# One overlapping transfer for eight shifted value tiles, a new order of the first loads, a third gate and up buffer, and zero matmuls between the first ones

## The chip, the cores and the metric

The kernel runs on one core of a Trainium2 chip. The core has five engines, each with its own instruction stream that runs in order: TensorE (PE; weight loads are listed apart as PEld), VectorE (DVE), ScalarE (ACT), GpSimd (POOL) and SyncE (SP), which here only issues transfers. The metric is the device time of one execution in microseconds (us), as the median of six runs.

## The reference

Sequence 2048, width D = 640, 32 heads of 20, window of 8 positions that lie 2 apart; F = 1536; bfloat16.

```python
xn = layernorm(x)                                  # (x - mean) / sqrt(var + 1e-5)
q, k, v = split(xn @ wqkv)                         # 32 heads of 20
logits[s, w] = q[s] . k[s - 2w] * 20**-0.5         # w = 0..7; s - 2w < 0 is masked out
o[s] = sum_w softmax_w(logits)[s, w] * v[s - 2w]
attention = o @ wo
glu = ((xn @ w_gate) * (xn @ w_up)) @ w_down       # bilinear: no nonlinearity
out = x + attention + glu
```

## The kernel before

The 2048 positions are 16 tiles of 128 (`tg`), in four chunks of four tiles (512 positions, `c`). All weights are loaded to SBUF once. For each chunk the stages are:

- `norm(c)`: DVE takes the statistics of each x tile (`stats`, `mv`), POOL makes 1/sigma (`rstd`), DVE scales (`xn`), PE turns the tile (`pst`) and ACT copies it to `xnT`. Chunk 0 goes tile by tile, so that on DVE the statistics of tile 2 stand ahead of `xn` of tile 1; the other chunks go by four tiles.
- `qk(c)` and `vproj(c)`: PE projects (`psqk`, `psv`), ACT copies to `qT`, `kT`, `v_t`. v goes out to a DRAM buffer `vD`, which begins with 14 rows of zeros (HALO). From there `load_v8(tg)` brings back, for each tile, eight copies of v, each shifted by two rows more, as one SBUF tile `v8` (two buffers).
- `weights(c)`: DVE multiplies q by eight shifted views of k (`pw`, eight products per chunk), PE sums over each head (`lps`), ACT takes the exponential (`e`).
- `attend(c)`: per tile PE turns the weights (`eT`), DVE normalises them (`rs`, `a`), multiplies the eight v copies by them (the mix, L481), and adds them up in three steps to `o`; PE turns `o` (`pso`), ACT copies it to `oT`.
- `glu(c)`: 12 column blocks f. For each, PE makes gate (`psg`) and up (`psu`), five matmuls each, ACT copies them to `gs` and `us` (two buffers each), DVE multiplies them to `hT`.
- `finish(c)`: per tile and half, PE adds attention output and down projection into `psf` (5 and 12 matmuls), DVE adds the residual `xr`, which POOL loads, into `osb`, and a transfer writes it out.

A hand-written list builder sets the order. `main` holds PE's stages and `chain` DVE's; `burst` and `quick` are short operations that are put in between when a table of estimated times says that they are ready. `later` holds transfers that are issued once a named step is done in that table (`want_v8`). The result is one fixed order per engine. On the chip an engine that waits holds back everything behind it in that order; SP too issues its transfers strictly in order. A name such as `v_599` is one buffer of `v8`, with a number that differs between tiles and between the two kernels.

Of the kernel before, what the change touches and what calls it, by code (L numbers as in the profile page):

```python
# [9 lines left out]
BF = dt.bfloat16  # L10
# [7 lines left out]
def kernel(  # L18
# [60 lines left out]
    def tcols(ttl):  # L79
        return slice(ttl * P, (ttl + 1) * P)  # L80
# [7 lines left out]

    x_tiles = {}

    def load_x(c):
        for ttl in range(CH):
            tg = c * CH + ttl
            x_t = cpool.tile([P, D], BF, name="x_t", bufs=6)
            nc.sync.dma_start(out=x_t[:], in_=x_flat[tg * P : (tg + 1) * P, :])
            x_tiles[tg] = x_t
# [7 lines left out]
            out=wqkv[:, :, r * D : (r + 1) * D], in_=wqkv_r[:, :, r * D : (r + 1) * D]  # L104
        )

    load_x(0)
    load_qkv(2)
    load_qkv(0)
    load_x(1)  # L110
    load_qkv(1)
# [20 lines left out]
    def constants():  # L132
        identity(P + H)
        for wl in range(JL):
            nc.gpsimd.affine_select(
                out=selb[:, P : P + H], in_=selb[:, P : P + H], pattern=[[-1, H]],
                compare_op=ALU.not_equal, fill=1.0, base=-H * wl, channel_multiplier=1,
            )
        nc.gpsimd.memset(Ek[:], 1.0)
        nc.gpsimd.affine_select(  # L140
            out=Ek[:], in_=Ek[:], pattern=[[P, KT], [-Dh, H]],
            compare_op=ALU.is_ge, fill=0.0, base=0, channel_multiplier=1,
        )
        nc.gpsimd.affine_select(
            out=Ek[:], in_=Ek[:], pattern=[[-P, KT], [Dh, H]],
            compare_op=ALU.is_ge, fill=0.0, base=Dh - 1, channel_multiplier=-1,
        )
        nc.gpsimd.memset(vmask[:], 1.0)
        for w in range(1, W):
            g, wl = divmod(w, JL)  # L150
            nc.gpsimd.memset(vmask[wl * H : (wl + 1) * H, g, 0 : DIL * w], 0.0)
        zt = cpool.tile([P, D], BF, name="zt", tag="osb")
        nc.gpsimd.memset(zt[0:HALO, :], 0.0)
        nc.gpsimd.dma_start(out=vD[0:HALO, :], in_=zt[0:HALO, :])
# [9 lines left out]
            nc.sync.dma_start(out=wo_perm[jl * H : (jl + 1) * H, :, :], in_=wo_r[jl])  # L164
        nc.sync.dma_start(out=wd[:], in_=B_w_down.rearrange("(f p) d -> p f d", p=P))

    wps = ps_log.tile([P, CS], F32, name="wps", tag="lg")
    for k in range(42):
        nc.tensor.matmul(wps[:, 0:P], lhsT=warm[:], rhs=warm[:], start=True, stop=True)

    INF = 1e9
    LAG = 0.2
# [53 lines left out]
    def norm(c, group):  # L226
        st = state[c]
        st["xnT"] = None

        def alloc():  # L230
            if st["xnT"] is None:
                st["xnT"] = cpool.tile([P, KT, CS], BF, name="xnT", bufs=3)

        def steps(t0):
            g = {}

            def stats():
                g["mv"] = cpool.tile([P, group, nc.vector.BN_AGGR_DIM], F32, name="mv", bufs=2)
                for k in range(group):
                    x_t = x_tiles[c * CH + t0 + k]  # L240
                    s = cpool.tile([P, 2, nc.vector.BN_STATS_DIM], F32, name="stats")
                    for hf in range(2):
                        nc.vector.bn_stats(s[:, hf, :], x_t[:, hf * N2 : (hf + 1) * N2])  # L243
                    nc.vector.bn_aggr(g["mv"][:, k, :], s[:])
                rstd = cpool.tile([P, group], F32, name="rstd", bufs=2)
                nc.gpsimd.tensor_scalar(rstd[:], g["mv"][:, :, 1], EPS, None, op0=ALU.add)
                nc.gpsimd.tensor_tensor(
                    rstd[:], rstd[:], mhalf[:].to_broadcast([P, group]), ALU.pow
                )
                g["rstd"] = rstd  # L250

            def stats_after(t):
                on("pool", ("rstd", c, t0), t + LAG, 0.85)

            op(chain, ("stats", c, t0), stats, 1.12 * group, None, stats_after)

            def scaling(ttl, k):
                def scale_x():
                    xn_t = cpool.tile([P, D], BF, name="xn_t")
                    nc.vector.tensor_scalar(  # L260
                        xn_t[:], x_tiles[c * CH + ttl][:],
                        scalar1=g["mv"][:, k, 0:1], scalar2=g["rstd"][:, k : k + 1],
                        op0=ALU.subtract, op1=ALU.mult,
                    )
                    st["xn", ttl] = xn_t

                def turn():
                    alloc()
                    pst = ps_tr.tile([P, KT, P], BF, name="pst", tag="tr")
                    for i in range(KT):  # L270
                        nc.tensor.transpose(  # L271
                            pst[:, i, :], st["xn", ttl][:, i * P : (i + 1) * P], ident
                        )
                    nc.scalar.copy(st["xnT"][:, :, tcols(ttl)], pst[:])

                def turned(t):
                    on("act", ("xnT", c, ttl), t + LAG, 0.7)

                def scaled(t):
                    op(burst, ("turn", c, ttl), turn, 0.3, when(("xn", c, ttl)), turned,  # L280
                       ("tr", ("xnT", c, ttl)), 0.5)

                def later_free():
                    old = ("turn", c, ttl - 2)
                    return max(done.get(("rstd", c, t0), INF), done.get(old, INF) if ttl >= 2 else 0.0)

                op(chain, ("xn", c, ttl), scale_x, 0.43, later_free, scaled)

            return [lambda k=k: scaling(t0 + k, k) for k in range(group)]

        if group == 1:
            prev = None
            for t0 in range(CH):
                cur = steps(t0)
                if prev:
                    prev[0]()
                prev = cur
            prev[0]()
        else:
            for t0 in range(0, CH, group):  # L300
                for f in steps(t0):
                    f()
# [70 lines left out]
    def load_v8(tg):  # L373
        c, ttl = divmod(tg, CH)
        v8 = apool.tile([P, W, D], BF, name="v8")
        for w in range(W):
            r0 = HALO + tg * P - DIL * w
            nc.sync.dma_start(out=v8[:, w, :], in_=vD[r0 : r0 + P, :])
        state[c]["v8", ttl] = v8
        done["v8", tg] = max(done["v", c, ttl, 1] + 2.5, done.get(("add1", tg - 2), 0.0)) + 5.0  # L380

# [5 lines left out]
    def weights(c):  # L387
        st = state[c]
        for g in range(2):
            for j in range(JL):  # L390

                def product(g=g, j=j):
                    off = HALO - DIL * (JL * g + j)
                    pt = apool.tile([P, KT, CS], BF, name="pw", tag="pw", bufs=6)
                    nc.vector.tensor_tensor(  # L395
                        pt[:], st["qT"][:], st["kT"][:, :, off : off + CS], ALU.mult
                    )
                    st["pw", g, j] = pt
# [28 lines left out]
    def attend(c, ttls):  # L427
# [29 lines left out]
        for ttl in ttls:  # L457
# [44 lines left out]
            def turn(ttl=ttl):  # L502
                o16 = st["o16", ttl]
                pso = ps_tr.tile([P, KT, P], BF, name="pso", tag="tr")
                for i in range(KT):
                    nc.tensor.transpose(pso[:, i, :], o16[:, i * P : (i + 1) * P], ident)  # L506
                oT = cpool.tile([P, KT, P], BF, name="oT", bufs=6)
                nc.scalar.copy(oT[:], pso[:])  # L508
                st["oT", ttl] = oT

# [1 line left out]
                on("act", ("oT", tg), t + LAG, 0.7)  # L512

            def mixed(t, tg=tg, turn=turn, turned=turned):
                old = ("pe fin", (tg - 6), 1)
                need = when(("add1", tg), *([old] if tg >= 6 else []))
                op(burst, ("turn o", tg), turn, 0.3, need, turned, ("tr", ("oT", tg)), 0.5)
                want_v8(tg + 2)

# [7 lines left out]
    def glu(c):  # L527
        st = state[c]
        for f in range(FT):
            for r in range(2):  # L530

                def emit(f=f, r=r):
                    w = wu if r else wg
                    ps = mm_tile("psu" if r else "psg")
                    for i in range(KT):
                        nc.tensor.matmul(  # L536
                            ps[:], lhsT=w[:, i, f * P : (f + 1) * P], rhs=st["xnT"][:, i, :],
                            start=(i == 0), stop=(i == KT - 1),
                        )
                    s = cpool.tile([P, CS], BF, name="us" if r else "gs", bufs=2)  # L540
                    nc.scalar.copy(s[:], ps[:])  # L541
                    st["gu", r, f] = s

# [10 lines left out]
                        op(quick, ("h", c, f), gate, 0.42, when(("gu", c, f, 1)))  # L554

                n = c * FT + f - 14
                need = [("h", c, f - 2)] if f >= 2 else []
                op(main, ("pe gu", c, f, r), emit, 1.08, when(*need), after, ("mm", ("gu", c, f, r)))

    def finish(c):  # L560
# [62 lines left out]
    )  # L623
    norm(1, 4)
    weights(0)
    side(lambda: (want_v8(0), want_v8(1), load_x(3)))
    norm(2, 4)
    attend(0, range(CH))
    weights(1)
    norm(3, 4)  # L630
    attend(1, range(CH))
# [52 lines left out]
```

## Time and profile before

| what | value |
|---|---|
| median of six runs | 289.16 us (287.37 to 290.72) |
| profiled execution | 288.73 us, span 287.0 us |
| granted TensorE clock, mean | 0.987 |
| moved by DMA | 40.96 MB, mean 143 GB/s |

The span runs from the first to the last instruction of the program; the rest of the execution's time lies around it. In lists of waits the columns are: who waited, for whom, us in total, times, longest. In timelines: start, duration, engine, line, operation, tiles, shapes, count, and in brackets the idle time ahead of it with what ended it. A group of matmuls shows a duration somewhat longer than its place in the stream, since the next group begins before its last results are out; the distance from start to start tells what it takes. In rows of windows the columns are the stretch, its length, the busy time of PE, PEld, DVE, ACT and POOL (with counts), the granted clock, the busy share of the DMA engines and GB/s.

### The profile page before, as it was taken

What the parts mean: (1) busy time and instruction counts of PE and PEld (TensorE: products, weight loads), DVE (VectorE), ACT (ScalarE), POOL (GpSimd) and SP (SyncE); (2) the same over time, 40 slices, a digit from 0 to 9 for tenths busy, and PEclk for the clock granted to TensorE, in tenths of its full rate; (3) what the DMA queues carried; (4) which work ended last, traced back from release to release, by engine and by line L of the source; (5) the groups of instructions that cost most, each with busy time, mean ns of one, the idle gap of its engine ahead of it and who ended that gap; (6) DMA issues with size and microseconds to landing.
All of it is one profiled execution on the core that took longest, in us unless ns stands there. A gap on an engine that the chain in (4) does not pass through costs nothing.

```text
span 287.0 us, 4601 instructions
## 1 busy us (share of the span) xinstructions
PE 273.9 (95%) x1778; PEld 155.1 (54%) x1778; DVE 197.6 (69%) x278; ACT 118.5 (41%) x209; POOL 34.7 (12%) x80
## 2 busy tenths in 40 slices
PE   7799999949999999999999999999999999999994
PEld 6554446514444577744444576654445775444773
DVE  5630894199999839999995996995999931211221
ACT  2466555624565521055555640025554003555000
POOL 4710004000000142100000041120000122000100
PEclk9799999997999999999999999999999999999999
DMA  6959993926666122776600485860066022000111
GB/s 212 337 174 382 280 312 119 315 75 183 184 185 183 48 69 70 216 223 202 182 4 3 123 270 178 252 206 26 0 181 188 23 74 88 0 0 2 43 51 47
DMA packets 30758, 40.96 MB, mean 143 GB/s; under 512 B 3298, under 2 KB 29424, under 8 KB 30736
## 3 DMA queue, kind: packets, MB, share of 16 engines
q1 hardware_dynamic: 28736, 33.93, 38.4%
q0 software_dynamic: 2000, 6.74, 7.1%
q8 instruction: 14, 0.23, 0.3%
q14 instruction: 8, 0.07, 0.1%
HBM read 35.39 MB, written 5.26 MB: 142 GB/s over the span
## 4 chain that ended last, share of the span: by engine, by line
PE 62%; DVE 26%; DMA 7%; issue 2%; SPq 1%; ACT 1%; POOL 1%; DVEq 0%; ACTq 0%
PE psf L584 14%; PE psqk L325 11%; PE psg L536 10%; PE psu L536 10%; PE psv L351 6%; PE psf L577 6%; DVE pw L395 5%; PE lps L406 3%; DMA wqkv<-in_A_wqkv_dram 2%; DVE hT L546 2%; DMA v_599<-vD 2%; DMA xr<-in_A_x_dram 2%; PE pst L271 1%; DVE osb L591 1%; DVE stats L243 1%
## 5 line engine op out<-in xcount | busy, mean ns | idle before, releaser
L536 PE MATMUL psg<-xnT,wg 128*128 128x512 bf16 x240 | 60.7, 384 | 0.0
L536 PE MATMUL psu<-xnT,wu 128*128 128x512 bf16 x240 | 59.9, 380 | 0.0
L584 PE MATMUL psf<-wd,hT 128*128 128x320 bf16 x384 | 57.7, 299 | 0.5 <-DVE hT L546 0.5
L395 DVE TENSOR_TENSOR pw<-qT,kT 128x2560 bf16<-128x2560 bf16 x32 | 46.0, 1484 | 0.7 <-PE lps L406 0.7
L584 PEld LDWEIGHTS <-hT 128*128 128x128 bf16 x384 | 37.5, 98 | 15.3 <-DVE hT L546 0.8
L541 ACT CAST gs<-psg 128x512 bf16<-128x512 f32 x48 | 28.2, 588 | 40.6 <-PE psg L536 32.5
L325 PE MATMUL psqk<-xnT,wqkv 128*128 128x512 bf16 x200 | 44.8, 379 | 0.0
L546 DVE TENSOR_TENSOR hT<-gs,us 128x512 bf16<-128x512 bf16 x48 | 20.2, 420 | 27.3 <-ACT us L541 27.3
L536 PEld LDWEIGHTS <-wu 128*128 128x128 bf16 x240 | 23.3, 98 | 27.7 <-issue 1.7
L541 ACT CAST us<-psu 128x512 bf16<-128x512 f32 x48 | 28.3, 589 | 24.1 <-PE psu L536 24.1
L536 PEld LDWEIGHTS <-wg 128*128 128x128 bf16 x240 | 23.4, 99 | 26.7 <-issue 1.2
L591 DVE TENSOR_TENSOR osb<-psf,xr 128x320 bf16<-128x320 f32 x32 | 15.3, 487 | 26.1 <-PE psf L584 17.0
L325 PEld LDWEIGHTS <-wqkv 128*128 128x128 bf16 x200 | 19.2, 98 | 22.4 <-issue 0.8
L351 PE MATMUL psv<-wqkv,xnT 128*128 128x320 bf16 x160 | 24.7, 310 | 2.4 <-DMA wqkv<-in_A_wqkv_dram 2.4
L577 PE MATMUL psf<-wo_perm,oT 128*128 128x320 bf16 x160 | 27.0, 299 | 0.0
L508 ACT COPY oT<-pso 128x640 bf16<-128x640 bf16 x16 | 11.1, 696 | 35.5 <-PE pso L506 35.5
L351 PEld LDWEIGHTS <-xnT 128*128 128x128 bf16 x160 | 15.7, 101 | 9.8 <-issue 2.8
L601 POOL DMA_DIRECT2D out_dram<-osb x13 | 7.1, 546 | 105.5 <-DVE osb L591 105.5
L577 PEld LDWEIGHTS <-oT 128*128 128x128 bf16 x160 | 15.3, 98 | 5.7
L357 ACT CAST v_t<-psv 128x320 bf16<-128x320 f32 x32 | 13.5, 427 | 11.7 <-PE psv L351 9.4
L363 POOL DMA_DIRECT2D vD<-v_t x12 | 6.7, 559 | 93.4 <-ACT v_t L357 93.3
L331 ACT CAST qT<-psqk 128x512 bf16<-128x512 f32 x20 | 11.8, 588 | 9.8 <-PE psqk L325 9.8
(136 smaller groups left out, 236.4 us busy)
## 6 DMA issues: line engine op xcount, KB each, us to landing
x_t<-in_A_x_dram SPq DMA_DIRECT2D x16, 160.0 KB, 7.1
xr<-in_A_x_dram POOLq DMA_DIRECT2D x16, 160.0 KB, 2.7
wqkv<-in_A_wqkv_dram SPq DMA_DIRECT2D x3, 800.0 KB, 7.4
out_dram<-osb POOLq DMA_DIRECT2D x13, 160.0 KB, 2.1
wg<-in_B_w_gate_dram SPq DMA_DIRECT2D x2, 960.0 KB, 7.2
wu<-in_B_w_up_dram SPq DMA_DIRECT2D x2, 960.0 KB, 9.3
wd<-in_B_w_down_dram SPq DMA_DIRECT2D x1, 1920.0 KB, 11.8
vD<-v_t POOLq DMA_DIRECT2D x12, 160.0 KB, 2.4
```

Of the source, the lines that this page charges most:

```text
L325: nc.tensor.matmul(ps[:], lhsT=wqkv[:, i, r * D + j * P : r * D + (j + 1) * P], rhs=st["xnT"][:, i, :], start=(i == 0), stop=(i == KT - 1),)
L331: nc.scalar.copy(dst[:, j, o : o + CS], ps[:])
L351: nc.tensor.matmul(ps[:, 0:N2], lhsT=st["xnT"][:, i, tcols(ttl)], rhs=wqkv[:, i, 2 * D + n0 : 2 * D + n0 + N2], start=(i == 0), stop=(i == ...
L357: nc.scalar.copy(v_t[:].rearrange("p (j h) -> p j h", j=Dh)[:, :, k * HH : (k + 1) * HH], ps[:, 0:N2].rearrange("p (h j) -> p j h", j=Dh),)
L395: nc.vector.tensor_tensor(pt[:], st["qT"][:], st["kT"][:, :, off : off + CS], ALU.mult)
L508: nc.scalar.copy(oT[:], pso[:])
L536: nc.tensor.matmul(ps[:], lhsT=w[:, i, f * P : (f + 1) * P], rhs=st["xnT"][:, i, :], start=(i == 0), stop=(i == KT - 1),)
L541: nc.scalar.copy(s[:], ps[:])
L546: nc.vector.tensor_tensor(h[:], st["gu", 0, f][:], st["gu", 1, f][:], ALU.mult)
L577: nc.tensor.matmul(ps[:, 0:N2], lhsT=st["oT", ttl][:, i, :], rhs=wo_perm[:, i, n0 : n0 + N2], start=(i == 0), stop=False,)
L584: nc.tensor.matmul(ps[:, 0:N2], lhsT=st["hT", f][:, tcols(ttl)], rhs=wd[:, f, n0 : n0 + N2], start=False, stop=(f == FT - 1),)
L591: nc.vector.tensor_tensor(osb[:, n0 : n0 + N2], ps[:, 0:N2], xr[:, n0 : n0 + N2], ALU.add)
```

## The change

- `load_v8` fetches the eight shifted copies by one transfer with an overlapping source pattern (128 rows x 8 shifts x 640) instead of eight transfers. Shift number w now is the one of 14 - 2w rows back, so the views of k and the mask of the first 14 positions run in the opposite order. The bytes moved are the same.
- The first loads: of chunk 0's x tiles two go ahead of the V third of wqkv and two behind it; before, all four went ahead.
- Chunk 3's x tiles are loaded behind attention 0 on the chain instead of ahead of normalisation 2.
- `gs` and `us` have three buffers instead of two (the builder holds gate and up of block f until `hT` of f - 3 instead of f - 2), `oT` five instead of six.
- `warm_up(n)`: the 42 matmuls of zeros at the start stay, and 14 more of the same kind follow the first turned tile.

```diff
-    def load_x(c):
-        for ttl in range(CH):
+    def load_x(c, ttls=range(CH)):
+        for ttl in ttls:
...
-    load_x(0)
+    load_x(0, (0, 1))
     load_qkv(2)
+    load_x(0, (2, 3))
     load_qkv(0)
     load_x(1)
     load_qkv(1)
...
-        for w in range(1, W):
+        for w in range(W - 1):
             g, wl = divmod(w, JL)
-            nc.gpsimd.memset(vmask[wl * H : (wl + 1) * H, g, 0 : DIL * w], 0.0)
+            nc.gpsimd.memset(vmask[wl * H : (wl + 1) * H, g, 0 : HALO - DIL * w], 0.0)
...
+    def warm_up(n):
+        wps = ps_log.tile([P, CS], F32, name="wps", tag="lg")
+        for k in range(n):
+            nc.tensor.matmul(wps[:, 0:P], lhsT=warm[:], rhs=warm[:], start=True, stop=True)
+    warm_up(42)
...
                     nc.scalar.copy(st["xnT"][:, :, tcols(ttl)], pst[:])
+                    if c == ttl == 0:
+                        warm_up(14)
...
-        for w in range(W):
-            r0 = HALO + tg * P - DIL * w
-            nc.sync.dma_start(out=v8[:, w, :], in_=vD[r0 : r0 + P, :])
+        rows = vD[tg * P : (tg + 1) * P, :]
+        nc.sync.dma_start(
+            out=v8[:],
+            in_=bass.AP(tensor=rows.tensor, offset=rows.offset, ap=[[D, P], [DIL * D, W], [1, D]]),
+        )
...
-                    off = HALO - DIL * (JL * g + j)
+                    off = DIL * (JL * g + j)
...
-                oT = cpool.tile([P, KT, P], BF, name="oT", bufs=6)
+                oT = cpool.tile([P, KT, P], BF, name="oT", bufs=5)
...
-                    s = cpool.tile([P, CS], BF, name="us" if r else "gs", bufs=2)
+                    s = cpool.tile([P, CS], BF, name="us" if r else "gs", bufs=3)
...
-                need = [("h", c, f - 2)] if f >= 2 else []
+                need = [("h", c, f - 3)] if f >= 3 else []
...
     weights(0)
-    side(lambda: (want_v8(0), want_v8(1), load_x(3)))
+    side(lambda: (want_v8(0), want_v8(1)))
     norm(2, 4)
     attend(0, range(CH))
+    side(lambda: load_x(3))
     weights(1)
```

How the order of instructions moves. On SP behind the other weights (wo_perm and wd are those of the output and down projections), before:

```order
L164 DMA wo_perm<-in_A_wo_dram 32x5x640 x4
L165 DMA wd<-in_B_w_down_dram 128x12x640
L95 DMA x_t<-in_A_x_dram 128x640 x4
L378 DMA v_599<-vD 128x640 x8
L378 DMA v_608<-vD 128x640 x8
```

and after:

```order
L165 DMA wo_perm<-in_A_wo_dram 32x5x640 x4
L166 DMA wd<-in_B_w_down_dram 128x12x640
L383 DMA v_606<-vD 128x8x640
L383 DMA v_608<-vD 128x8x640
L383 DMA v_849<-vD 128x8x640
L383 DMA v_933<-vD 128x8x640
L383 DMA v_1009<-vD 128x8x640
L383 DMA v_1085<-vD 128x8x640
L95 DMA x_t<-in_A_x_dram 128x640 x4
```

Chunk 3's four x loads moved from ahead of the first v8 transfer to behind the sixth (tile 5, `v_1085`), and each tile is one transfer.

On DVE, where the statistics of chunk 3 end and finish 0 begins, before:

```order
L244 BN_AGGR mv<-stats 128x2
L260 TENSOR_SCALAR xn_t<-x_t,mv,rstd 128x640 x2
L591 TENSOR_TENSOR osb<-psf,xr 128x320 x2
L260 TENSOR_SCALAR xn_t<-x_t,mv,rstd 128x640 x2
L463 RECIPROCAL rs<-eT 128x32
```

and after:

```order
L248 BN_AGGR mv<-stats 128x2
L599 TENSOR_TENSOR osb<-psf,xr 128x320
L264 TENSOR_SCALAR xn_t<-x_t,mv,rstd 128x640
L599 TENSOR_TENSOR osb<-psf,xr 128x320
L264 TENSOR_SCALAR xn_t<-x_t,mv,rstd 128x640
L599 TENSOR_TENSOR osb<-psf,xr 128x320
L264 TENSOR_SCALAR xn_t<-x_t,mv,rstd 128x640 x2
```

The residual additions, which need `xr`, moved ahead of the scalings of chunk 3.

On DVE in finish 1, where the first residual addition stands, before (the mix of tile 10, `v_1975`):

```order
L463 RECIPROCAL rs<-eT 128x32
L465 TENSOR_TENSOR a_2077<-eT,rs 128x256
L481 TENSOR_TENSOR v_1975<-v_1975,a_2077 128x5120
L496 TENSOR_TENSOR v_1975<-v_1975 128x2560
L591 TENSOR_TENSOR osb<-psf,xr 128x320
```

and after (the mix of tile 9, `v_1709`):

```order
L471 RECIPROCAL rs<-eT 128x32
L473 TENSOR_TENSOR a_1978<-eT,rs 128x256
L489 TENSOR_TENSOR v_1709<-v_1709,a_1978 128x5120
L504 TENSOR_TENSOR v_1709<-v_1709 128x2560
L504 TENSOR_TENSOR v_1709<-v_1709 128x1280
L599 TENSOR_TENSOR osb<-psf,xr 128x320
```

The first residual addition of finish 1 now comes about one tile of attention earlier in DVE's order.

More of the change, by code (lines that the diff above doesn't have):

```diff
@@ L165, in load_down @@
         nc.sync.dma_start(out=wd[:], in_=B_w_down.rearrange("(f p) d -> p f d", p=P))
-    wps = ps_log.tile([P, CS], F32, name="wps", tag="lg")
-    for k in range(42):
-        nc.tensor.matmul(wps[:, 0:P], lhsT=warm[:], rhs=warm[:], start=True, stop=True)
+    def warm_up(n):
[3 more added lines that the diff above has]
+    warm_up(42)
     INF = 1e9
@@ L514, in mixed @@
             def mixed(t, tg=tg, turn=turn, turned=turned):
-                old = ("pe fin", (tg - 6), 1)
-                need = when(("add1", tg), *([old] if tg >= 6 else []))
+                old = ("pe fin", (tg - 5), 1)
+                need = when(("add1", tg), *([old] if tg >= 5 else []))
                 op(burst, ("turn o", tg), turn, 0.3, need, turned, ("tr", ("oT", tg)), 0.5)
```

## The prediction

> **What bounds the kernel now.** I read the page first (span, busy shares, slices), then the waits, then the timeline around each place where PE stands still.
>
> ```profile
> span 287.0 us, 4601 instructions
> PE 273.9 (95%) x1778; PEld 155.1 (54%) x1778; DVE 197.6 (69%) x278; ACT 118.5 (41%) x209; POOL 34.7 (12%) x80
> PE   7799999949999999999999999999999999999994
> ...
> PEclk9799999997999999999999999999999999999999
> ```
>
> TensorE (PE) is busy 95% of the span; a slice is 7.2 us. Two places stand out: the first two slices, and the ninth with the tenth (57 to 72 us), where PE falls to 4 and the clock to 7. A microsecond is won where PE waits or runs at a lower clock. The waits name what is behind it; SP's own are the last row.
>
> ```profile
> ACT gs L541 <- DVE hT L546: 7.9, 5, 4.9
> DVE v_599 L481 <- DMA v_608<-vD: 4.9, 1, 4.9
> ...
> SPq L95 <- DVE xn_t L260: 14.2, 4, 12.2
> ```
>
> The timeline from 32 us shows how these belong together:
>
> ```profile
> 32.13 15.52 SPq L95 DMA_DIRECT2D x_t<-in_A_x_dram  x4
> 47.70 4.05 SPq L378 DMA_DIRECT2D v_599<-vD  x8
> 52.48 0.42 DVE L465 TENSOR_TENSOR a_784<-eT,rs 128x256 bf16<-128x256 f32 x1
> 57.50 1.24 PE L536 MATMUL psg<-xnT,wg 128*128 128x512 bf16 x5
> 57.85 2.83 DVE L481 TENSOR_TENSOR v_599<-v_599,a_784 128x5120 bf16<-128x5120 bf16 x1 [4.95 <-DMA v_608<-vD]
> 58.58 1.24 PE L536 MATMUL psu<-xnT,wu 128*128 128x512 bf16 x5
> 61.10 0.59 ACT L541 CAST gs<-psg 128x512 bf16<-128x512 f32 x1 [4.92 <-DVE hT L546]
> 65.04 2.34 PE L536 MATMUL psg<-xnT,wg 128*128 128x512 bf16 x5
> 68.48 1.24 PE L536 MATMUL psg<-xnT,wg 128*128 128x512 bf16 x5
> 124.75 0.44 PE L506 MATMUL pso<-selb,o_1566 128*128 128x128 bf16 x5
> 125.03 0.23 PE L439 MATMUL eT<-selb,e 128*128 128x160 bf16 x1
> 125.17 1.24 PE L536 MATMUL psu<-xnT,wu 128*128 128x512 bf16 x5
> ```
>
> SP stands 15.5 us on chunk 3's x loads, whose buffers chunk 2's normalisation frees. Behind them wait the first eight V rows (v_599), issued from 47.70. DVE has its factor a_784 at 52.90 and waits for them until 57.85. The gate product hT stands behind that mix on DVE, the gs copy on ACT behind hT, and PE behind them all.
>
> **The change, part by part.** *Chunk 3's x behind attention 0; one transfer per tile.* SP then issues v_606 and v_608 (tiles 0 and 1) right behind the down weights (wd), near 32 us. What a transfer takes:
>
> ```profile
> wd<-in_B_w_down_dram SPq DMA_DIRECT2D x1, 1920.0 KB, 11.8
> L378 SPq DMA_DIRECT2D v_846<-vD x8: 319/430/432, 64.0 to 67.2; - x8
> L481 DVE TENSOR_TENSOR v_846<-v_846,a_940 x1: 2819/2819/2819, 72.1 to 72.1; 128x5120 bf16<-128x5120 bf16 x1
> DMA to landing us min/median/max: 2.2/3.2/3.4
> q1 hardware_dynamic: 1152, 1.31, 67.3%
> L378 SPq DMA_DIRECT2D v_1975<-vD x8: 319/430/432, 160.7 to 163.9; - x8
> L481 DVE TENSOR_TENSOR v_1975<-v_1975,a_2077 x1: 2825/2825/2825, 167.9 to 167.9; 128x5120 bf16<-128x5120 bf16 x1
> ```
>
> The q1 row is the window 64 to 70.5 us: one tile is 1.31 MB and takes 0.673 x 6.5 = 4.4 us of all DMA engines. With wd landed near 31.4 + 11.8 = 43.2, tile 0 is there by about 47.6 and tile 1 by 52. They are wanted near 51.6 and 59. So the 4.95 us go, with some 4 us of room. What PE lost there: from psu at 58.58 to psg at 68.48 it did three groups of five (57.50 to 58.58: 1.08 each), one pso (124.75 to 125.03: 0.28) and an eT pair (0.14), 3.66 us of work in 9.90. **Term 1: -6.2 us.** Of it about 1.3 is the lower clock behind the standstill (the psg from 65.04 took 2.1 instead of 1.08).
>
> Later tiles: a transfer starts when its buffer comes free and has until its mix 8.1 us (64.0 to 72.1), in the tightest case 7.2 (160.7 to 167.9). Eight pieces took 67.2 + 3.2 - 64.0 = 6.4. One piece needs no eight issues: between 4.4 + 2.2 (engine time and the smallest landing) = 6.6 and wd's 11.8. I take 6.6, since the v8 rows are of the same packets and wd's landing ran beside other loads. Cost nothing while the 7.2 covers it; the upper end is a rival. Chunk 3's x now stands behind v_1085, whose buffer the last tile of attention 0 frees: some 6.6 us later the tiles are there, and eight products (1484 ns each in the groups, 11.9 us) stand on DVE before the statistics. Hidden by about 3 us.
>
> *First loads.* Start of the timeline:
>
> ```profile
> 0.79 1.81 SPq L95 DMA_DIRECT2D x_t<-in_A_x_dram  x4
> 1.05 4.66 PE L169 MATMUL wps<-warm 128*128 128x128 bf16 x42 [1.05 <-DVE warm L114]
> 2.64 1.00 SPq L103 DMA_DIRECT2D wqkv<-in_A_wqkv_dram  x2
> 5.65 0.88 DVE L243 BATCH_NORM_STATS2 stats<-x_t 128x6 f32<-128x320 bf16 x2
> 5.79 0.63 PE L271 MATMUL pst<-selb,xn_t 128*128 128x128 bf16 x5
> 6.69 0.39 DVE L260 TENSOR_SCALAR xn_t<-x_t,mv,rstd 128x640 bf16<-128x640 bf16 x1
> 8.04 0.41 DVE L260 TENSOR_SCALAR xn_t<-x_t,mv,rstd 128x640 bf16<-128x640 bf16 x1
> 8.81 0.84 PE L351 MATMUL psv<-wqkv,xnT 128*128 128x320 bf16 x5 [2.39 <-DMA wqkv<-in_A_wqkv_dram]
> 13.34 3.56 PE L351 MATMUL psv<-wqkv,xnT 128*128 128x320 bf16 x25
> 16.74 3.40 PE L325 MATMUL psqk<-xnT,wqkv 128*128 128x512 bf16 x15
> 10.00:13.00 3.00, 3.00 (x16) 1.94 (x15) 2.09 (x6) 1.92 (x4) 2.47 (x14) 0.50 1.07 361
> DMA to landing us min/median/max: 6.1/7.4/7.9
> ```
>
> The V third of wqkv is issued two x tiles (2 x 0.45) sooner and lands near 7.9 instead of 8.8. The 14 zero matmuls at 4.66 / 42 = 0.11 each run from 6.42 to 7.97, so the first psv starts at 8.0 either way. The 2.4 us in which PE stood still are closed, and I expect the half clock of the window 10 to 13 (0.50) to go with them.
>
> Against it stands x tile 2, now behind V: its statistics (5.65) stand on DVE ahead of xn of tile 1 (6.69). If it lands as now, PE runs dense from 8.0: eight psv of 0.68 (3.40 / 5) and three pst of 0.28 (as pso), 6.3, so psqk starts at 14.3, a gain of 2.4. If it lands with V near 7.8, xn of tile 1 comes at 7.8 + 1.04 = 8.85, of tile 2 1.35 later, of tile 3 about 1 us after that; the last pst ends near 12.0 and with 3.40 of psv psqk starts at 15.4, a gain of 1.3. The landing row is the three wqkv thirds: the first-issued took 6.1 and the second, issued half a microsecond later, 7.9; transfers land in the order of issue. I take **term 2: -1.3 us**.
>
> The Trainium skill, "DMA: Bandwidth & Descriptors", section "Queues, rings and completion order", says that each DMA engine consumes a queue's descriptors in ring order; that speaks against this reorder, the landings of V and Q agree, and by it term 2 is 1.3, by a free order 2.4. "TensorE: Matmul & The Clock Gate", Part 1, lowers the clock after an idle window of about 3.4 us; here 2.4 us without matmuls was enough, so the row decides. By the page the lower clock need not go with this gap; that case is the third rival.
>
> *Third gs and us buffer, fifth oT buffer.* They let PE run one more pair of groups (2.16 us) ahead of DVE. With the mix on time the two buffers hardly waited elsewhere (7.9 us in five waits, 4.9 of them here), so I cost this at nothing. oT with five: tile 5 waits for tile 0's last product, which is done before; nothing.
>
> *Order of DVE and PE behind it.* The new list puts osb ahead of xn in finish 0 and moves attention of chunks 1 and 2 about a tile later against PE. Places where PE or DVE now wait:
>
> ```profile
> 106.85 0.89 DVE L591 TENSOR_TENSOR osb<-psf,xr 128x320 bf16<-128x320 f32 x2 [3.07 <-DMA xr<-in_A_x_dram]
> 176.64 0.45 PE L506 MATMUL pso<-selb,o_2149 128*128 128x128 bf16 x5 [0.62 <-DVE o_2149 L493]
> ```
>
> With osb first, DVE's wait for xr (3.07) delays xn too, and the pst behind it may hold PE by up to the two osb, 0.9. In finish 1 three pso follow one another closely; each may wait as the one above did, 3 x 0.62 = 1.9. That 0.62 itself may go instead. So between -0.6 and +2.8. I take **term 3: +0.2**, near the lower end, because in the row of before only one of these places waited, and DVE gains nearly as much ahead of them (4.95 and the earlier start) as PE.
>
> **Sum.** 287.0 - 6.2 - 1.3 + 0.2 = 279.7 span. The profiled execution took 288.73, 1.73 around its span: 281.4. It lay 0.43 under the median of the six runs (289.16), so 281.9.
>
> **Rivals.** *One piece is slow* (slower). One transfer keeps less in flight than eight, or overlapping rows cost. It decides from about 9 us: eight tiles (two per chunk, whose buffer is freed a tile before) then wait 0.9 each and the gain is gone. At wd's 11.8 about 3.7 each; where DVE is full, six of eight pass on to PE, 22 us: 304. For: wd; against: 4.4 us of engine time, and 361 GB/s in the row 10 to 13, where two thirds of wqkv and a few x tiles were open. Chance 0.09.
>
> *DVE becomes the bound.* It gains the 4.95 us and loses them nowhere, but PE's 6.2 and 1.3 come only where DVE follows; if PE waits at lps or pso with DVE's time, the gain is 4.95: 284.2. For: from the groups, DVE's mixes and products fill it through the attention stages; against: behind 70 us PE's longest wait on DVE is the 0.62 above. Chance 0.10.
>
> *The start gains nothing*: tile 2 later still, or the half clock all the same (half of the 3 us in the row 10 to 13): 281.9 + 1.5 = 283.4. For: PE still has holes of some 0.6 us behind the first psv; against: the half clock followed a standstill four times as long. Chance 0.07.
>
> *The change doesn't free the first mix*: wd and the other loads hold v_606 to 55 or later. Then only the third buffer helps (2.16) and the start: 289.2 - 2.2 - 1.3 = 285.7; with the start lost too, 287 to 288.5. For: 1.9 MB ahead; against: 4 us of room. Chance 0.06.
>
> The likeliest, all terms about as given, has 0.68: 279.5 to 283.
>
> **How the numbers follow.** Lower end: term 2 at 2.4 and term 3 at -0.6: 281.9 - 1.1 - 0.8 = 280.0, and 1.0 for what a median of runs with a spread of 3.4 may move: 279.0. Upper: DVE as the bound, 284.2, and the same 1.0: 285.2. What lies outside is slow transfers, most of a late v_606 and the tail, under 2 in 10. 0.5% is 1.45 us, about what these runs (287.4 to 290.7) can tell from no change. Faster: 0.68 + 0.10 + 0.07 + 0.02 = 0.87; the rest of the late v_606 is no change, 0.04; slower 0.09.
>
> **What would show it.** Right: no DVE wait on vD near 50, PE busy without a hole at 55 to 70 and its clock 1.0 there, v8 landings of 6 to 7 us, psqk from about 15.4, no half clock at 10 to 13. Wrong: DVE waits on vD at several tiles, landings over 9, or PE waits on pw, pso or pst that add up to more than 3 us.

## The result, and the profile after

The changed kernel takes 281.88 us (median of ten runs, 280.93 to 282.84); the kernel before, run beside it, 289.02 us (20 runs, 287.37 to 290.72). The ratio is 0.9758, with a 95% interval of 0.9735 to 0.9781: faster by 7.1 us. The forecast was 281.9. The ratios here and below leave out executions that were disturbed on the chip, the medians do not, so a ratio can differ a little from that of two medians.

The page of the changed kernel (a slice is 7.0 us):

```profile
span 280.5 us, 4461 instructions
PE 271.3 (97%) x1792; PEld 154.3 (55%) x1792; DVE 197.7 (71%) x278; ACT 118.8 (42%) x209; POOL 34.6 (12%) x80
PE   8699999799999999999999999999999999999995
PEclk9999999999999999999999999999999999999999
```

The hole of slices nine and ten is gone, and so are both stretches of lower clock. The windows of the changed kernel show the same (columns as in the windows before: PE, PEld, DVE, ACT, POOL, granted clock, DMA share, GB/s). TensorE (PE) is busy for all of 55 to 70 us; but in 10 to 13 us it now has gaps, and from 40 to 50 us the DMA engines are full.

```profile
10.00:13.00 3.00, 2.69 (x28) 1.68 (x25) 2.20 (x7) 2.42 (x5) 2.31 (x8) 1.00 0.81 211
40.00:50.00 10.00, 9.59 (x81) 5.79 (x80) 5.66 (x18) 3.73 (x8) 2.96 (x5) 1.00 1.02 354
55.00:70.00 15.00, 15.00 (x78) 7.12 (x76) 14.86 (x20) 9.09 (x16) 0.00 (x0) 1.00 0.27 90
```

A new dip stands in the eighth slice, where PE shows a 7. The timeline from 32 to 54 us tells what it is:

```profile
32.31 2.56 SPq L383 DMA_DIRECT2D v_606<-vD  x1
34.91 4.91 SPq L383 DMA_DIRECT2D v_608<-vD  x1
44.20 0.24 POOL L250 TENSOR_SCALAR rstd<-mv 128x4 f32<-128x4 f32 x1 [25.88 <-DVE mv L248]
45.52 1.73 POOL L369 DMA_DIRECT2D vD<-v_t  x3
46.71 1.24 PE L544 MATMUL psg<-xnT,wg 128*128 128x512 bf16 x5
48.35 1.24 PE L544 MATMUL psu<-xnT,wu 128*128 128x512 bf16 x5
50.83 0.75 ACT L363 CAST v_t<-psv 128x320 bf16<-128x320 f32 x2 [4.85 <-DMA vD<-v_t]
51.30 1.24 PE L544 MATMUL psg<-xnT,wg 128*128 128x512 bf16 x5 [1.71 <-ACT v_t L363]
52.72 0.44 PE L275 MATMUL pst<-selb,xn_t 128*128 128x128 bf16 x5 [0.18 <-ACT xnT L278]
```

ScalarE (ACT) wants a buffer for chunk 1's fourth v tile. `v_t` has three; they come free when their writes to `vD` have landed, and those writes, issued by GpSimd (POOL) from 45.52, share the DMA engines with the two early v8 transfers. ACT waits 4.85 us. Behind the copies that wait, in ACT's order, stand those of gate and up and of `xnT`, so PE loses 1.87 us ahead of psg (51.30 less 48.35 + 1.08) and 0.34 us ahead of pst (52.72 less 51.30 + 1.08): 2.2 us.

The writes are late for a second reason, which the kernel before shares. The first of these v tiles lay ready at 41.96, but in POOL's order chunk 2's `rstd` stands ahead of the writes, and it waited for DVE's statistics until 44.20. The kernel before, at the same place:

```profile
46.29 1.73 POOL L363 DMA_DIRECT2D vD<-v_t  x3
48.80 0.75 ACT L357 CAST v_t<-psv 128x320 bf16<-128x320 f32 x2 [2.06 <-PE psg L536]
```

There the first write landed at 48.70, 2.4 us after its issue, just ahead of the copy at 48.80. So the copy was waiting for that landing, although the row names psg, and its 2.06 us cost PE nothing. In the changed kernel the first write took 5.2 us (45.52 to 50.73), and that difference is what reached PE. Issued at 41.96 and with the same 5.2 us, it would have landed near 47.2, an estimate; whether an earlier issue alone removes PE's loss was not tried.

So the span's -6.5 us comes about so: the hole -6.2, the start -0.8 (psqk at 15.98 instead of 16.74), the new wait +2.2, and -1.7 left over behind it.

The start, on PE and VectorE (DVE):

```profile
6.14 0.94 PE L171 MATMUL wps<-warm 128*128 128x128 bf16 x14
7.79 0.84 PE L357 MATMUL psv<-wqkv,xnT 128*128 128x320 bf16 x5 [0.70 <-DMA wqkv<-in_A_wqkv_dram]
8.22 0.89 DVE L247 BATCH_NORM_STATS2 stats<-x_t 128x6 f32<-128x320 bf16 x2 [2.54 <-DMA x_t<-in_A_x_dram]
9.72 0.45 PE L275 MATMUL pst<-selb,xn_t 128*128 128x128 bf16 x5 [1.09 <-DVE xn_t L264]
15.98 1.24 PE L331 MATMUL psqk<-xnT,wqkv 128*128 128x512 bf16 x5
```

x tile 2 landed just behind V, as the forecast took it, and PE paid 1.09 us for it. And the landings of the 16 v8 transfers, from the answer on the line that issues them (smallest, median and largest, in us):

```profile
DMA to landing us min/median/max: 5.2/6.2/16.0
```

The 16.0 is that of `v_608`, which queued behind the down weights. No mix waited for `vD`.

### The profile page after: what moved, and what is told of

It reads as the page before. It is cut to its first block, busy times and chain, and to the rows that moved or that the text cites. A ratio compares the mean times of both kernels' runs of the same rounds, so it can differ in the third digit from the quotient of the medians.

```text
span 280.5 us, 4461 instructions
## 1 busy us (share of the span) xinstructions
PE 271.3 (97%) x1792; PEld 154.3 (55%) x1792; DVE 197.7 (71%) x278; ACT 118.8 (42%) x209; POOL 34.6 (12%) x80
## 4 chain that ended last, share of the span: by engine, by line
PE 73%; DVE 11%; DMA 7%; issue 4%; POOL 2%; ACT 1%; SPq 0%; DVEq 0%; POOLq 0%; ACTq 0%
PE psu L544 18%; PE psg L544 17%; PE psf L592 12%; PE psqk L331 12%; PE psf L585 5%; DVE pw L403 4%; PE psv L357 4%; DMA xr<-in_A_x_dram 3%; DVE stats L247 3%; DMA x_t<-in_A_x_dram 2%; PE lps L414 2%; DMA vD<-v_t 2%; PE pso L514 1%; PE pst L275 1%; DVE v_2060 L489 1%
## 5 line engine op out<-in xcount | busy, mean ns | idle before, releaser
L544 PE MATMUL psg<-xnT,wg 128*128 128x512 bf16 x240 | 59.6, 379 | 1.7 <-ACT v_t L363 1.7
L357 PE MATMUL psv<-wqkv,xnT 128*128 128x320 bf16 x160 | 23.5, 299 | 0.7 <-DMA wqkv<-in_A_wqkv_dram 0.7
L247 DVE BATCH_NORM_STATS2 stats<-x_t 128x6 f32<-128x320 bf16 x32 | 13.6, 467 | 4.6 <-DMA x_t<-in_A_x_dram 4.6
```

Of the source, the lines that this page charges most:

```text
L357: nc.tensor.matmul(ps[:, 0:N2], lhsT=st["xnT"][:, i, tcols(ttl)], rhs=wqkv[:, i, 2 * D + n0 : 2 * D + n0 + N2], start=(i == 0), stop=(i == ...
L544: nc.tensor.matmul(ps[:], lhsT=w[:, i, f * P : (f + 1) * P], rhs=st["xnT"][:, i, :], start=(i == 0), stop=(i == KT - 1),)
```

## The experiments

Twelve kernels ran, in three groups of four; each group had the kernel before on the same chip, at 288.62, 288.71 and 287.61 us in order (21, 11 and 17 runs). Where an interval is given, it is that of the ratio to this. The first four are the kernel before with one part of the change each, the next four the changed kernel with one thing altered, the last four close what stayed open.

**Chunk 3's x loads alone.** The kernel before, with:

```diff
-    side(lambda: (want_v8(0), want_v8(1), load_x(3)))
+    side(lambda: (want_v8(0), want_v8(1)))
     norm(2, 4)
     attend(0, range(CH))
+    side(lambda: load_x(3))
```

> The kernel before with one part alone: chunk 3's x loads behind attention 0, so that the first V rows (eight pieces per tile) are issued near 32 us. If the late V rows are what opened the hole at 60 to 68 us, that hole (6.2 us) closes; the V rows then fill the DMA engines up to about 50 us and chunk 1's writes of v wait behind them as in the changed kernel, which costs about 2.2 near 49 us: 289.0 - 6.2 + 2.2 = 285.0, between 284.0 and 286.0. If instead one piece per tile is what brought the gain, 288.5 or more.

Measured: 285.12 us, ratio 0.9864 (0.9810 to 0.9917), -3.5 us. The first mix no longer waits, and the hole is gone. The profiled execution (283.07, mean clock 0.998) is one of the two quick ones of six; the other four took 284.8 to 287.2 at clocks of 0.987 to 0.992, so the median holds a lowered clock that this trace does not show. Three rows from the waits of this trace, behind 20 us:

```profile
PE pso L506 <- DVE o L493: 1.1, 2, 0.9
PE psg L536 <- ACT v_t L357: 0.7, 1, 0.7
PE psf L584 <- DVE hT L546: 0.6, 1, 0.6
```

The second is the new wait on `v_t`, smaller. The other two, PE waiting for DVE, are little larger than in the kernel before (0.8 and 0.5). So the wait on `v_t` comes with the early v8 transfers, in eight pieces too.

**One transfer per tile alone.** The kernel before, with `load_v8`, the views of k and the mask as in the change.

> The kernel before with one part alone: the eight shifted tiles by one transfer each, order of loads as before. The first transfer is still issued at 47.7 us and lands 6 to 8 us later, 54 to 55.5 instead of 57.85: the hole in PE shrinks from 4.4 to 1 to 2 us and the lower clock behind it may not come (1.3). 285.5, between 284.5 and 287.5. If the number of pieces does not matter, 289.0.

Measured: 290.87 us, ratio 1.0097 (1.0061 to 1.0134): slower, where 285.5 was expected. Its timeline (the first row merges four issues):

```profile
49.15 23.82 SPq L377 DMA_DIRECT2D v<-vD  x4
59.31 2.82 DVE L483 TENSOR_TENSOR v<-v,a 128x5120 bf16<-128x5120 bf16 x1 [4.99 <-DMA v<-vD]
65.52 0.72 PE L508 MATMUL pso<-selb,o 128*128 128x128 bf16 x5 [4.28 <-DVE o L495]
```

The first tile is there 10.16 us after its issue; in eight pieces it took 57.85 - 47.70 = 10.15 from the first issue. The hole is the old one, later by the 1.4 us that this execution's first matmuls were late. Fewer issues did not bring the rows sooner. Where the 2.2 us of the medians are lost is not settled: behind 70 us PE waits 2.3 us in two pso rows, where before it waited 0.8.

**The buffers alone.** The kernel before, with three `gs` and `us`, five `oT`, and the builder's rules that go with them.

> The kernel before with one part alone: three gs and us buffers, five oT buffers and the order that the builder makes of them. PE runs one more pair of groups (2.16 us) ahead into the hole; the lower clock behind a hole of 2.2 us may stay away (1.3); and the new order drops the waits of PE on DVE at lps, pso and psf (1.7 less in term 3 of the changed kernel): 289.0 - 2.2 - 1.3 - 1.7 = 283.8 at best; I expect 285.5, between 283.8 and 287. As the prediction priced it (nothing), 289.0.

Measured: 286.01 us, ratio 0.9924 (0.9883 to 0.9964), -2.6 us. PE's wait in the hole fell from 4.2 us to one row of its waits from 45 to 75 us:

```profile
PE pso L506 <- DVE o L493: 2.2, 1, 2.2
```

**The first loads and the zero matmuls alone.** The kernel before, with `load_x(0, (0, 1))` ahead of `load_qkv(2)`, `load_x(0, (2, 3))` behind it, and `warm_up(14)`.

> The kernel before with one part alone: the first loads reordered and 14 zero matmuls behind the first turned tile. The changed kernel's psqk starts 0.76 us sooner (15.98 against 16.74): 288.2. If the end does not follow the start, because the hole at 60 us is set by the V rows that SP holds back, 289.0.

Measured: 286.77 us, ratio 0.9943 (0.9908 to 0.9977), -1.9 us, more than expected. In its profile psqk begins at 14.86, no stretch at the start has a lower clock, and PE's longest wait in the hole is 3.2 us instead of 4.2; why the hole shrank was not followed up. Singly the four parts come to -3.5 + 2.3 - 2.6 - 1.9 = -5.7 us; together they gave -7.1.

**Four `v_t` buffers.** The changed kernel with:

```diff
-                        st["v_t"] = cpool.tile([P, D], BF, name="v_t", bufs=3)
+                        st["v_t"] = cpool.tile([P, D], BF, name="v_t", bufs=4)
...
-                    h = cpool.tile([P, CS], BF, name="hT", bufs=14)
+                    h = cpool.tile([P, CS], BF, name="hT", bufs=13)
```

> The changed kernel with four v_t buffers instead of three (and 13 hT buffers instead of 14, to make room). The order is the same. If the hole of 2.2 us near 49 us in the changed kernel comes from ACT's copy waiting for a v_t buffer whose write to DRAM is stuck behind the early V rows, it goes: 281.9 - 2.2 = 279.7, between 279.2 and 280.5. If the busy DMA engines hurt in another way (POOL's queue, the writes themselves), 281.9.

Measured: 279.40 us, ratio 0.9703 (0.9652 to 0.9754), and a span of 277.8 us, 2.7 less than the changed kernel's. The same place in its timeline:

```profile
46.51 0.42 ACT L363 CAST v_t<-psv 128x320 bf16<-128x320 f32 x1 [0.30 <-PE psv L357]
47.14 0.42 ACT L363 CAST v_t<-psv 128x320 bf16<-128x320 f32 x1 [0.21 <-PE psv L357]
49.66 1.24 PE L544 MATMUL psg<-xnT,wg 128*128 128x512 bf16 x5
```

ACT no longer waits for `vD`, and psg follows psu (48.58) after 1.08 us. Removing what made ACT wait removed the wait: that cause is shown. The order of instructions is that of the changed kernel. The ratio's interval lies below that of the changed kernel's second run (below, 0.9763 to 0.9828) and overlaps that of the first a little.

**No zero matmuls between the first ones.** The changed kernel without this:

```diff
-                    if c == ttl == 0:
-                        warm_up(14)
```

> The changed kernel without the 14 zero matmuls behind the first turned tile. If they keep the clock up, a window of 3.4 us at half clock comes back between 9 and 13 us and costs up to 1.7, less what the waits there hide: 282.9, between 282.4 and 283.6. If the clock falls only after an idle window of 3.4 us, nothing changes: 281.9.

Measured: 282.57 us, ratio 0.9810 (0.9767 to 0.9853). The interval overlaps the changed kernel's, so the time is not told apart. In its profile the half clock is back, at 8 to 12 us:

```profile
8.00:10.00 2.00, 1.30 (x6) 0.50 (x5) 1.47 (x5) 0.42 (x1) 0.29 (x1) 0.58 1.07 380
10.00:12.00 2.00, 2.00 (x14) 1.48 (x15) 1.27 (x4) 0.70 (x2) 1.44 (x5) 0.57 0.71 195
```

**All four x tiles ahead of V again**, in the changed kernel.

```diff
-    load_x(0, (0, 1))
+    load_x(0)
     load_qkv(2)
-    load_x(0, (2, 3))
```

> The changed kernel with the first loads in the order of before (all four x tiles ahead of V), zero matmuls kept. V lands near 8.8 as before, but x tile 2 near 5.4, so xn of tile 1 does not wait: PE runs dense from 8.8 and psqk starts at 8.8 + 6.3 = 15.1 instead of 15.98: 281.0, if the clock stays up over the 1.7 us without work ahead of 8.8. If it falls, 1.7 is lost again: 282.7. If the reorder is worth the 0.9 by which V lands sooner, 282.8.

Measured: 280.84 us, ratio 0.9775 (0.9714 to 0.9835). The median is 1.0 below the changed kernel's, the ratio is not: not told apart. Its six executions fall in two groups: four of 280.4 to 281.2 at a mean clock of 1.0, and two of 283.2 and 284.3 at 0.992 and 0.987.

**Eight transfers per tile again**, in the changed kernel.

```diff
+        for w in range(W):
+            r0 = tg * P + DIL * w
+            nc.sync.dma_start(out=v8[:, w, :], in_=vD[r0 : r0 + P, :])
```

> The changed kernel with eight transfers per tile instead of one, order otherwise as changed. Eight pieces took 6.4 to 7.3 from first issue to last landing, one piece 5.2 to 5.9 undisturbed and up to 8.6 beside other traffic; both lie under the about 8 us that each tile has. So no change: 281.9, between 281.2 and 282.8. If one piece is what holds the gain, 284 or more.

Measured: 280.76 us, ratio 0.9750 (0.9704 to 0.9796), the changed kernel's within the interval. One piece gains the kernel nothing here either. One of the six executions, the profiled one, had a mean clock of 0.992: in it the clock fell to 0.55 from 10 to 12 us, although the zero matmuls are there.

**Two `gs` and `us` buffers again**, in the changed kernel.

```diff
-name="us" if r else "gs", bufs=3)
+name="us" if r else "gs", bufs=2)
...
-                need = [("h", c, f - 3)] if f >= 3 else []
+                need = [("h", c, f - 2)] if f >= 2 else []
```

> The changed kernel with gs and us at two buffers each again, and the planner's rule on them at f - 2, so that the builder writes out another order. Theory A (the third buffer alone gained 2.6 us on the kernel before because the order that came of it shortened the hole in TensorE's work; the hole is gone here, so nothing is left to gain): 281.9 us, 281.5 to 282.3. Theory B (the stalls on lps, pso and psf behind 140 us, some 2.9 us before and 1.2 in the changed kernel, went with the order that three buffers give): they come back, 283.5 us, and the trace shows TensorE waiting for DVE at pso or psf for 2 us or more behind 125 us.

Measured: 284.99 us, ratio 0.9896 (0.9857 to 0.9935). The changed kernel unaltered, on the same chip, gave 281.88 and 0.9796 (0.9763 to 0.9828): the third buffer is worth 3.1 us where there is no hole. Theory B had the direction. Its own mark, 2 us of PE at pso or psf behind 125 us, was not met: PE's waits behind 70 us there come to 1.4.

```profile
PE psf L592 <- DVE hT L554: 1.0, 1, 1.0
PE lps L414 <- DVE pw L403: 0.4, 1, 0.4
```

In the unaltered one the only such row is pst, 0.3:

```profile
PE pst L275 <- DVE xn_t L264: 0.3, 1, 0.3
```

Its first psqk began at 16.82 and it ended 2.1 us sooner than this run, whose psqk began at 16.13: 2.8 us between the two. Rows of waits show 1.4 - 0.3 = 1.1 of it. Counted from start to start of PE's groups, delays of over 0.1 us behind 70 us come to 2.7 us in this run and 0.7 in the unaltered one, and two eT groups near 61 and 69 us stand 0.35 and 0.22 us late in this run alone: together about 2.5 of the 2.8.

**Four `v_t` buffers and the old loads together.**

> The changed kernel with v_t at four buffers (hT at 13) and all four x tiles of chunk 0 ahead of V again. If the two steps add as they came singly (279.40 and 280.84 against 281.88 of the changed kernel): 278.4 us. Rival (the order of the first loads is worth nothing either way, and the 1.0 us of that run was its interval's width): 279.4 us, no different from four buffers alone.

Measured: 280.39 us, ratio 0.9723 (0.9675 to 0.9771). The two do not add. Two of its six executions took 277.6, at mean clocks of 0.998 and 1.0, the other four 280.1 to 281.3, at 0.994; the profile is one of the first two. In it psv runs from 8.06 and psqk begins at 14.38, what the forecast had worked out for a PE that runs dense from 8.0:

```profile
8.06 0.84 PE L356 MATMUL psv<-wqkv,xnT 128*128 128x320 bf16 x5 [1.07 <-DMA wqkv<-in_A_wqkv_dram]
14.38 3.40 PE L330 MATMUL psqk<-xnT,wqkv 128*128 128x512 bf16 x14
```

Four `v_t` buffers with the new loads ran five of six times at 0.999 or 1.0. With the run of all four x tiles ahead of V, above, that makes 6 of 12 executions with the old order at 0.994 or less, against 2 of 35 with the new order (the changed kernel in both runs, four buffers, eight transfers, two buffers), all of them with the zero matmuls.

**The changed kernel again.**

> The changed kernel, unaltered, as the control for the runs beside it: 281.9 us. For its trace: first psqk matmul at 16.0 us after the span's start as in the first profile, if the late x tile 2 is a result of the order of the loads. Rival (the loads of the first 15 us land at another moment in each execution, whatever the order: the same start code of the kernel before began psqk at 14.85, 16.05, 16.74 and 18.16 us in four profiles): anything between 14.9 and 18.2 us, here more than 0.5 us from 16.0.

Measured: 281.88 us as before, ratio 0.9796 (0.9763 to 0.9828), against a kernel before that took 287.61 on this chip. Its psqk began at 16.82 instead of 15.98: the rival's mark.

**One piece and the late x loads**, in the kernel before.

> The kernel before with two edits: the transfer of eight shifted values in one piece, and the x loads of chunk 3 behind attention of chunk 0. Theory (one piece costs nothing by itself; what it lost alone, 290.87 us against 288.62, hung on the hole that chunk 3's x loads open): 285.1 us, as the x loads alone gave. Rival (one piece costs 2.2 us wherever it stands): 287.4 us. For the trace: no wait of DVE on vD over 2 us near 59 us by the first; waits of TensorE on pso near 178 and 187 us by the second, as in the run of one piece alone (0.78 and 1.53 us).

Measured: 286.13 us, ratio 0.9944 (0.9908 to 0.9981), between 285.1 and 287.4. The mix near 53 us does not wait for `vD`, as the theory said, but PE waits at pso as the rival said, and so did the run of the x loads alone (1.1 us, above) and, less, the kernel before (0.8):

```profile
PE pso L508 <- DVE o L495: 1.7, 2, 1.1
PE psg L538 <- ACT v_t L357: 1.7, 1, 1.7
```

What one piece costs without the third buffer stays open between 0 and 2.3 us; with it, it is nothing.

## Why the prediction was right, and where only its sum was

*Term 1, the hole, -6.2: right.* It went whole, with its lower clock, and through the step named. The `v_608` transfer landed 16.0 us after its issue from 34.91, at 50.9, near the 52 forecast.

*Missing: what the early transfers do to others, +2.2.* The prediction asked whether v8 would be in time behind the other weights, and never which transfers would now run beside them. The row to read stood in the profile: the DMA share of before, last but one in the window from 40 to 50 us, and two transfers of 4.4 us each moving in there:

```profile
40.00:50.00 10.00, 10.00 (x85) 6.04 (x83) 6.43 (x18) 5.39 (x13) 3.13 (x6) 1.00 0.50 164
```

With them the share was 1.02. Chunk 1's v writes lie in that window with three buffers. Four buffers took the wait away.

*Third buffer, priced at nothing: wrong by some 3 us.* The reason given was that waits of gs for hT were small outside the hole. But PE's program is written out ahead in an order for which the buffer count is one rule, and three buffers give another order. The same count of PE's delays behind 70 us, over all profiles, comes to 2.5 to 4.0 us in the six with two buffers and to 0.7 to 1.4 in the eight with three: fewer of PE's groups stand close behind the DVE work that they need. Removing the third buffer cost 3.1 us. From the kernel before to the changed one the count falls from 2.5 to 1.2, which is most of the -1.7 left over in the balance. The buffer and the order always changed together, so which of the two does it was not separated.

*Term 3, +0.2: the sign was wrong*, since the delays behind 70 us shrank by 1.3 instead. Of its feared waits the osb ahead of xn came true (0.7 us near 104 us, from the starts of PE's groups; 0.3 of it stands as a wait), the three pso only as one of 0.3.

*Term 2, the start, -1.3: not resolved, and its reasoning too sure.* The two profiles show -0.8. But over the seven profiles with all four x tiles ahead, psqk begins between 14.28 and 18.16 us (mean 15.7), and over the seven with two between 14.86 and 17.49 (mean 16.3). Start code that is the same to the letter (the kernel before, the x loads alone, one piece alone, buffers alone) began at 16.74, 14.85, 18.16 and 16.05. One profile's start is one draw from that, and both the term and the row it was read from were such draws. What the zeros and the new order hold together is the clock: it was 0.998 or more in all 17 executions of the changed kernel and at most 0.994 in all 49 of the kernel before (there the hole lowers it too). In the kernels without the hole the mean clock was 0.994 or less in 2 of 35 executions with both, in 6 of 12 with the zeros alone, in 5 of 6 with the new order alone, and in 13 of 18 with neither (the x loads alone, and with one piece). In time little of this is resolved: without the zeros the median was 0.7 us higher, with the old loads 1.0 lower, both within the intervals.

*One piece, hidden: right*, for the changed kernel. The median landing was 6.2 (6.6 taken), the largest after the two early ones 8.6, and no mix waited. The rival "slow" is out: its 9 us were passed by the two early transfers alone.

So the mechanism of the largest term held; the rest of the sum did not. The total came out to the tenth by luck: two omissions of opposite sign, +2.2 and the third buffer's gain (-1.7 in this balance, 3.1 where it was taken out), nearly cancelled.

The version with the lowest median is the changed kernel with four `v_t` buffers: 279.40 us, ratio 0.9703.

## What to carry to other kernels

When a transfer is moved earlier, read the DMA share of the window that it moves into and list the buffers whose release waits on a transfer there; the engine that fills them is the next to wait. Look also at when such a transfer is issued: work that waits ahead of it in the issuing engine's order delays it too. Where a program's order is planned from buffer counts, a buffer is a change of order, and its price is to be read from the groups that stand close behind their producers, not from the wait for the buffer alone. A term read from the first microseconds of one profile needs several profiles before it is a number.

## What the runs showed of the hardware

*The same gap lowers the clock in one execution and not in another.* With the same start code PE stood still 2.17 us ahead of the first psv in the profile of the x loads alone, and 2.08 us in that of the buffers alone. Clock over 5 to 16 us of the first, then the psv of both:

```profile
5.00:16.00 11.00, 8.78 (x72) 6.28 (x72) 7.66 (x24) 5.65 (x12) 7.18 (x27) 1.00 0.92 322
8.54 0.84 PE L351 MATMUL psv<-wqkv,xnT 128*128 128x320 bf16 x5 [2.17 <-DMA wqkv<-in_A_wqkv_dram]
...
8.31 1.49 PE L351 MATMUL psv<-wqkv,xnT 128*128 128x320 bf16 x5 [2.08 <-DMA wqkv<-in_A_wqkv_dram]
```

Five psv took 0.84 us in the one and 1.49 in the other. The prediction said that 2.4 us "was enough, so the row decides"; it was enough once. The Trainium skill, "TensorE: Matmul & The Clock Gate", Part 1, has the window run freely, without a reset at the kernel's start, and the same kernel differ from run to run; these two rows agree with that, though gaps shorter than its 3.4 us suffice here.

*The clock column can miss a lowered clock.* In the profile of one piece alone the windows from 8 to 16 us all show 1.00, while five psv from 10.09 took 1.49 us instead of 0.84:

```profile
10.00:12.00 2.00, 1.91 (x11) 1.32 (x11) 0.00 (x0) 0.39 (x1) 1.62 (x10) 1.00 1.07 366
10.09 1.49 PE L351 MATMUL psv<-wqkv,xnT 128*128 128x320 bf16 x5 [3.60 <-DMA wqkv<-in_A_wqkv_dram]
```

The duration of like matmuls is the surer sign. The counts of executions by mean clock, above, can therefore miss a few.

*One large transfer was about a microsecond quicker than eight, and the kernel gained nothing by it.* From the first issue to the last landing the 14 tiles behind 60 us took 6.4 to 8.4 us in the kernel before (median 7.1), 6.6 to 10.2 in the changed kernel with eight pieces (6.9), and 5.2 to 8.6 with one (6.0). For the first tile, in traffic, it was 10.16 us against 10.15 from issue to use. The Trainium skill, "DMA: Bandwidth & Descriptors", "Rules for kernel authors", advises to coalesce many small transfers into one large one; at 160 KB apiece the transfer gains that microsecond, and the whole kernel nothing that these runs show.

*An issue can hold its engine for long.* `v_608` took SP 4.91 us to issue; transfers of the same shape later in the program took 0.36. That the full queue ahead of it is the reason was not tried.
